# Attention, Fourier mixing and a feed-forward layer on one core: clearing tiles behind the fourth head, loading mask rows first, and copying kept columns in one step

## The chip, the core and the metric

The kernel runs on one core of a Trainium2 chip. A core has five engines with instruction streams of their own: TensorE (PE in the profile) multiplies matrices, and the loads of its stationary operand are listed apart as PEld; VectorE (DVE), ScalarE (ACT) and GpSimd (POOL) do elementwise work; SyncE (SP) only issues transfers. Each engine works through its own stream in order. Transfers between the device's memory and the on-chip memory are carried by 16 DMA engines; here they are issued from the streams of SP, ACT and POOL. The metric is the time of one execution on the device in microseconds; lower is better.

## The reference

Softmax attention with a block-causal mask over 8 batches of 8 heads, 576 positions of 64 columns; then a Fourier mixing over positions and over the 512 columns, of which the real part is added to the input; then a normalization and a feed-forward layer with 2048 hidden units:

```python
scores = scale * np.matmul(q, k.transpose(0, 1, 3, 2))
mask = block_i >= block_j                      # blocks of 64 positions
scores = np.where(mask, scores, -1000000000.0)
attn = np.exp(scores - np.max(scores, axis=-1, keepdims=True))
attn = attn / (np.sum(attn, axis=-1, keepdims=True) + 1e-09)
attn_out = np.matmul(attn, v)
...
x = np.ascontiguousarray(attn_out.transpose(0, 2, 1, 3)).reshape(B, S, H * D)
X = np.fft.fft(x, axis=1)
X = np.fft.fft(X, axis=2)
u = x + np.real(X)
mu = np.mean(u, axis=-1, keepdims=True)
var = np.mean((u - mu) ** 2, axis=-1, keepdims=True)
un = (u - mu) / np.sqrt(var + 1e-06)
out = u + np.maximum(un @ w_ch1, 0.0) @ w_ch2
```

q, k and v have the shape (8, 8, 576, 64); w_ch1 is 512 x 2048, w_ch2 is 2048 x 512; everything is float32.

## The kernel before

**How precision is kept.** Most products are made of two half-precision parts of each operand, a high and a low one. The weights' parts are made on the chip: the weights are loaded as they are (tile `W`, lines 1403 to 1427), DVE takes their bits apart in three passes (`weight_single`, line 1430), ACT sums their squares into a spare tile called `left` for a scale, and later steps scale and split them.

**The lanes and the planner.** The kernel is written as lanes of steps (`Step`, line 160): one lane loads heads, others prepare them, find maxima, make scores, make values, transform a finished batch, load the weights, and so on. A step has a function that emits instructions, a TensorE cost, a chain of the engines that it uses with a modelled cost of each, the steps that it must come after, and a place. A planner at the end (lines 1609 to 1675) picks steps in turn, keeps a model of when each engine is free (`Queue`, line 179; a step is booked in the first gap that its cost fits in) and emits each part of a step at its modelled start. The streams follow this order exactly, since every instruction is kept in program order (`Ordered`, line 203, and `mm`, line 245). So each stream's order is fixed when the kernel is built, and modelled costs decide it.

**A head.** For a head h, the transposed queries and keys stand in a tile `lead` (rows 0 to 63), below them nine more rows: eight mask rows and one row for the maxima. For the first two heads (`HF` = 2) this is `LEAD[h]`, whose rows 64 to 72 are loaded from `c_masks` by POOL's queue at line 317. `max_part` (line 659) multiplies over 72 rows, DVE reduces the maxima into `M`, `shift` (line 717) turns them by a product with the identity `ident`, ACT copies the result into `mt`, and SP's queue writes it into row 72 of `lead`. `scores` (line 747) then multiplies over 73 rows, so that mask and maximum are part of the product. ACT makes the exponentials `p` and their high part `ph`, POOL the low part `pl`; `values` (line 779) multiplies them with v, and DVE divides by the sums `DEN` (lines 815 to 820). A score step of a head needs parts of the values of the head before it (line 837).

**A batch.** When the eight heads of a batch are through, `fourier_steps` (line 873) transforms it. `mirror` loads the batch's rows as they are (`X`) and mirrored (`U`); `folded` adds and subtracts halves; `stage1` (line 943) multiplies with the cosine and sine tables over positions into tiles `z`; `stage1_tail` does one more column into `ZT`. The second stage, `stage2_sin` and `stage2_cos` (lines 987 and 1004), works on three pieces c = 0, 1, 2 of the transformed positions. Pieces 0 and 1 have 128 positions each and read the `z` tiles. Piece 2, the last 33 positions, is made for two batches at once: every batch copies its last columns of `z` and `ZT` into the kept tiles `ZP` and `ZTP`, at column offset `o`, 0 for even and 64 for odd batches (lines 961 and 979). Every odd batch then runs piece 2 for both batches, from `ZP` and `ZTP`, into `X2` and `U2`. The columns between the two batches' parts in the kept tiles are zero; they are cleared once, at the start: `X2` and `U2` by POOL (lines 312 and 313), `ZTP` and the eight halves of `ZP` by DVE (lines 323 to 326).

After the second stage `normalized_steps` (line 1080) normalizes 256 rows at a time and turns them, and `feed_steps` (line 1168) runs the feed-forward layer, which TensorE works on whenever no lane has a step ready.

**The tables.** `table_lane` (line 1601) loads the Fourier tables in four pieces, behind the values of heads 1, 2, 4 and 5 (`TABLES = (1, 2, 4, 5)`, line 45). Heads are counted from 0.

Of the kernel before, what the change touches and what calls it, by code (L numbers as in the profile page):

```python
# [9 lines left out]
F32 = mybir.dt.float32  # L10
# [3 lines left out]
AF = mybir.ActivationFunctionType  # L14
ALU = mybir.AluOpType
# [4 lines left out]
B, H, S, D = 8, 8, 576, 64  # L20
# [12 lines left out]
HF = 2  # L33
# [11 lines left out]
TABLES = (1, 2, 4, 5)  # L45
# [18 lines left out]
KS = KM + 1  # L64
# [155 lines left out]
def tile_attn_fourier_ffn(  # L220
# [31 lines left out]


    ident_r = const.tile([P, P], F32R, name="ident")
    gpsimd.dma_start(ident_r, c_id)
    ident = ident_r.bitcast(F32)
    rows = const.tile([P, 3], I32, name="rows")
    sync.dma_start(rows, c_rows)
    ones = const.tile([P, P], F32, name="ones")
# [4 lines left out]
    o = [0]  # L264
# [39 lines left out]
    VH = [const.tile([P, 5, 2, D + 1], F16, name=f"VH_{i}") for i in range(2)]  # L304
    VL = [const.tile([P, 5, 2, D], F16, name=f"VL_{i}") for i in range(2)]
    ZT = const.tile([P, NCOS], F32R, name="ZT")
    for i in range(2):
        gpsimd.memset(MAIN[i], LEAST)
        gpsimd.memset(MAIN[i][0:64, 0:1], 0.0)
        gpsimd.memset(DIAG[i], LEAST)  # L310
    X2, U2 = (const.tile([P, DM], F32, name=x) for x in ("X2", "U2"))
    gpsimd.memset(X2, 0.0)
    gpsimd.memset(U2, 0.0)
    ZP = {(name, m): const.tile([P, 2, width], F32R, name=f"zp{name}{m}") for name, width in (("c", 98), ("s", 96)) for m in range(2)}
    ZTP = const.tile([P, 98], F32R, name="ztp")
    for i in range(HF):
        gpsimd.dma_start(LEAD[i][D:KS], c_masks)
        vector.tensor_scalar(LEAD[i][0:D, 0:64], ones[0:D, 0:64], 0.0, None, op0=ALU.mult)
    for i in range(2):
        vector.memset(VH[i][:, 0:4, :, D:D + 1], 1.0)  # L320
        vector.memset(VH[i][0:64, 4, :, D:D + 1], 0.0)
        vector.memset(VH[i][64:128, 4, :, D:D + 1], 1.0)
    vector.tensor_scalar(ZTP, ones[:, 0:98], 0.0, None, op0=ALU.mult)
    for t in ZP.values():
        for x in range(2):
            vector.tensor_scalar(t[:, x], ones[:, 0:t.shape[2]], 0.0, None, op0=ALU.mult)
    for at in range(0, NCOS, P):
        w = min(P, NCOS - at)
        vector.tensor_scalar(ZT[:, at:at + w], ones[:, 0:w], 0.0, None, op0=ALU.mult)
# [543 lines left out]
    def fourier_steps(b):  # L873
# [59 lines left out]
        z = {}  # L933
# [9 lines left out]
        def stage1(name, m):  # L943
            mat, stack, k2, n = MATS[name]
            f0, f1, f2 = (fs[name, c] for c in range(3))
            ds = slice(P * m, P * (m + 1))
            t = ps_tile()
            i = 0
            for c, f in enumerate((f0, f1)):
                for a, w in ((0, 0), (1, 0), (0, 1)):  # L950
                    mm(t[:, 0:n], f[:, a, ds], mat[:, c, w], start=(i == 0), stop=False)
                    i += 1
            mm(t[:, 0:n], f2[0:k2, ds], stack[0:k2], start=False, stop=True)
            yield
            zz = z[name, m] = ztile(name, m).rearrange("p (x n) -> p x n", x=2)
            scalar.copy(zz[:, 0], t[:, 0:n])
            yield
            vector.tensor_tensor(zz[:, 1], t[:, 0:n], zz[:, 0].bitcast(F32), op=ALU.subtract)
            yield
            w = 33 if name == "c" else 32  # L960
            scalar.copy(ZP[name, m][:, :, o:o + w], zz[:, :, 256:256 + w].bitcast(F32))
            yield

        def stage1_tail():
            mat, stack, k2, n = MATS["c"]
            f0, f1, f2 = (fs["c", c] for c in range(3))
            t = ps_tile()
            i = 0
            for c, f in enumerate((f0, f1)):
                for w in range(2):  # L970
                    mm(t[0:2, 0:n], f[:, :, LDH], mat[:, c, w], start=(i == 0), stop=False, skip_group_check=True)
                    i += 1
            mm(t[0:1, 0:n], f2[0:k2, LDH:LDH + 1], stack[0:k2], start=False, stop=True, skip_group_check=True)
            yield
            scalar.copy(ZT[0:2], t[0:2, 0:n])
            yield
            vector.tensor_tensor(ZT[32:34], t[0:2, 0:n], ZT[0:2].bitcast(F32), op=ALU.subtract)
            yield
            scalar.copy(ZTP[:, o:o + 33], ZT[:, 256:289].bitcast(F32))
            yield  # L980

        bss = {}
# [4 lines left out]
        def stage2_sin(c):  # L987
            n = 128 if c < 2 else 96
            t = ps_tile()
            i = 0  # L990
            ns = slice(P * c, P * c + n)
            for m in range(2):
                for a, w in ((0, 0), (0, 1), (1, 0)):
                    lhs = z["s", m][:, a, ns] if c < 2 else last("s", m, a)
                    mm(t[0:n, 0:KCOL], lhs, sd[:, m, w], start=(i == 0), stop=(i == 5))
                    i += 1
            yield
            bs = bss[c] = work.tile([P, KCOL], F32, name="bs", bufs=1)
            if c == 2:
                gpsimd.memset(bs[96:97], 0.0)  # L1000
            scalar.copy(bs[0:n], t[0:n, 0:KCOL])
            yield

        def stage2_cos(c):
# [27 lines left out]
        D_ = lambda *a: ("d", b) + a  # L1032
        place = H * (b + 0.9)
        yield Step(
            mirror, 0.0, ("L3.0", "P3", "L2.5"), (("V", H * b + H - 1, 4),) + ((("F", feed_number(b - 2, 1)),) if b > 1 else ()), D_("u"),
            place=place,
        )
        def folds(name, op, width):
# [6 lines left out]
        def stages(name):  # L1045
            for m in range(2):
                yield Step(
                    lambda m=m: stage1(name, m), 0.87, ("A0.42", "D0.47", "A0.25"), (D_("f" + name),),
                    D_("z" + name) if m == 1 else None, True, place=place,
                )  # L1050
            if name == "c":
                yield Step(stage1_tail, 0.62, ("A0.4", "D0.46", "A0.23"), (D_("fc"),), D_("zt"), True, place=place)

        cos, sin = ("c", ALU.add, 257), ("s", ALU.subtract, 256)
        order = (folds(*cos), folds(*sin), stages("c"), stages("s"))
        for steps in order:
            yield from steps
        def second_stage(c):
            yield Step(lambda: stage2_sin(c), 0.67, ("A0.38",), (D_("zs"),), D_("b", c), True, place=place)
            yield Step(  # L1060
                lambda: stage2_cos(c), 0.78, ("D0.86", "B", "G3.0"), (D_("zc"), D_("zt"), D_("b", c)) + ((("F", feed_number(3, 2)),) if c == 2 and b == 5 else ()), D_("u", c), True,
                place=place,
            )

        for c in range(2):
            yield from second_stage(c)
        uu = tuple(D_("u", c) for c in range(3))
        yield from normalized_steps(low, uu[0:2], (store(b, 0), store(b, 1)), place)
        if b % 2:
# [84 lines left out]
    def feed_number(b, i):  # L1154

        return 2 * b + 1 + b // 4 + i
# [435 lines left out]
    def load_table(i):  # L1592

        ends = (0, 4 * NCOS, 4 * NCOS + 4 * NSIN, 5 * NCOS + 5 * NSIN + 4 * KCOL, c_dft.shape[1])
        lo, hi = ends[i], ends[i + 1]
        vector.tensor_scalar(dft[0:1, lo:lo + 1], DEN[i % 2][0:1, 0:1], 0.0, None, op0=ALU.mult)
        yield
        gpsimd.dma_start(dft[:, lo:hi], c_dft[:, lo:hi])
        yield

    def table_lane():
        for i in range(4):
            yield Step(lambda: load_table(i), 0.0, ("D0.15", "P1.0", "M2.3"), (("V", TABLES[i], 4),), ("dft", i), place=TABLES[i])

    def transform_lane():
# [114 lines left out]
```

## Time and profile before

| What | Value |
|---|---|
| median of 3 runs | 1207.31 us |
| lowest and highest of them | 1205.13 us, 1212.7 us |
| the profiled execution | 1204.48 us |
| its span in the profile | 1202.3 us |
| mean granted clock of TensorE over it | 0.965 of full speed |

The span is the time from the first to the last recorded instruction. In the lines of the profile, a line in order of time gives the start, the duration, the engine, the source line, the operation, what it writes and reads, and how many instructions are merged in it; in brackets stand the idle time of the engine before it and what ended that idle time. A line with L213 or L246 names a helper through which all instructions of an engine go, so the tiles' names tell what the work is. A waiting table's line says who waited for whom: microseconds in all, how often, and the longest. In a line on one tile, the three numbers after the count are the shortest, median and longest duration in nanoseconds, then come the first and the last start. A queue's line gives packets, megabytes and the time of its packets as a share of the 16 DMA engines: q1 is SP's queue, q10 ACT's, q0 POOL's. An issue of a transfer ("DMA_DIRECT2D") is the time of the issuing engine alone, not of the transfer. POOL's durations are rough.

### The profile page before, as it was taken

The page shows a single profiled execution, that of the slowest core. Times are in us where ns is not written, and L with a number is a line of the kernel's source. Part 1 is how long each engine was busy: PE and PEld are TensorE (multiplying, and loading weights), DVE is VectorE, ACT ScalarE, POOL GpSimd, SP SyncE. Part 2 cuts the span into 40 slices and gives each one's busy share as a digit, 9 for nine tenths or more (in the row PEclk, how much of TensorE's full clock was granted, in tenths as well). Part 3 has the DMA queues.
Part 4 walks back from the last instruction along what each step waited for, and adds up shares of the span by engine and source line. Part 5 has one row for each costly group of instructions (what it writes and reads, how often), then busy time and mean ns, then how long its engine had stood idle before and what let it go on. Part 6 is the DMA issues. An engine that isn't in the chain of part 4 may idle for free.

```text
span 1202.3 us, 26143 instructions
## 1 busy us (share of the span) xinstructions
PE 1122.9 (93%) x10182; PEld 824.4 (69%) x10182; DVE 741.8 (62%) x1616; ACT 630.8 (52%) x1374; POOL 475.6 (40%) x621
## 2 busy tenths in 40 slices
PE   4767799998789999999999999999999999999998
PEld 3544475675566777777776767677766766888875
DVE  6886876557857576666665566666656434454431
ACT  5666759757756566556574654675222212334320
POOL 4552414544653254425442533353334210455410
PEclk9956989999889999999999999999999999999999
DMA  9687233443444234543435422360122021011100
GB/s 259 194 253 233 105 106 87 121 124 103 123 115 103 76 87 106 113 132 81 123 99 142 126 82 82 91 151 14 32 43 56 23 60 30 28 36 26 28 19 18
DMA packets 94049, 115.07 MB, mean 96 GB/s; under 512 B 37591, under 2 KB 64129, under 8 KB 93926
## 3 DMA queue, kind: packets, MB, share of 16 engines
q1 hardware_dynamic: 86582, 89.06, 28.2%
q10 hardware_dynamic: 4384, 16.78, 4.3%
q0 software_dynamic: 2960, 7.58, 2.3%
q8 instruction: 80, 1.31, 0.5%
q14 instruction: 43, 0.35, 0.1%
HBM read 58.50 MB, written 18.89 MB: 64 GB/s over the span
## 4 chain that ended last, share of the span: by engine, by line
PE 70%; DVE 1%; DMA 1%; ACT 0%; SPq 0%; issue 0%; POOL 0%; DVEq 0%; ACTq 0%; POOLq 0%
PE acc L246 24%; PE ps L246 23%; PE h L246 17%; PE av L246 6%; DMA lead<-mt 1%; DMA rest<-lead 0%; SPq L213 0%; DVE p L213 0%; PE ps L249 0%; DVE M L213 0%; DVE gl L213 0%; ACT p L213 0%; DVE st L213 0%; DVE x L213 0%; PE h L249 0%
## 5 line engine op out<-in xcount | busy, mean ns | idle before, releaser
L213 POOL TENSOR_TENSOR pl<-p,ph 128x288 f16<-128x288 f32 (+1 forms) x256 | 261.0, 1029 | 345.6 <-ACT ph L213 188.3
L246 PEld LDWEIGHTS <-W 128*128 128x128 f16 x3456 | 332.5, 98 | 60.4 <-issue 1.5
L246 PE MATMUL acc<-W,gh 128*128 128x512 f16 (+1 forms) x1008 | 289.5, 369 | 1.5 <-DVE W L213 1.2
L246 PE MATMUL ps<-uh,W 128*128 128x256 f16 x1184 | 217.6, 273 | 0.0
L246 PE MATMUL h<-uh,W 128*128 128x256 f16 x1120 | 207.7, 275 | 0.0
L246 PE MATMUL acc<-W,gl 128*128 128x512 f16 (+1 forms) x504 | 186.2, 370 | 1.0 <-DVE gl L213 1.0
L246 PE MATMUL ps<-ul,W 128*128 128x256 f16 x592 | 161.2, 272 | 0.0
L246 PE MATMUL h<-ul,W 128*128 128x256 f16 x560 | 153.8, 275 | 0.1
L246 PEld LDWEIGHTS <-ph 128*128 128x128 f16 x2112 | 132.4, 102 | 27.1 <-issue 4.6
L246 PEld LDWEIGHTS <-gh 128*128 128x128 f16 x1056 | 98.8, 98 | 69.5 <-issue 1.8
L246 PE MATMUL av<-VH,pl 128*128 128x65 f16 (+1 forms) x963 | 117.2, 201 | 19.1 <-POOL pl L213 16.4
L213 DVE TENSOR_REDUCE M<-ps 128x1 fp32r<-128x320 f32 (+4 forms) x214 | 96.1, 483 | 59.7 <-PE ps L246 53.9
L246 PE MATMUL ps<-lead 73*128 73x288 f16 (+10 forms) x494 | 115.9, 295 | 14.1 <-DMA lead<-in_c_masks_dram 10.3
L246 PE MATMUL av<-VH,ph 128*128 128x65 f16 (+1 forms) x966 | 119.2, 202 | 3.2 <-DVE x L213 2.6
L246 PEld LDWEIGHTS <-pl 128*128 128x128 f16 x1056 | 102.9, 101 | 24.4 <-POOL pl L213 20.4
L246 PE MATMUL av<-VL,ph 128*128 128x64 f16 x960 | 117.4, 200 | 0.0
L213 ACT ACTIVATE gh<-ps 128x512 f16<-128x512 f32 x74 | 44.0, 594 | 114.8 <-PE ps L246 114.8
L213 ACT CAST ph<-p 128x512 f16<-128x512 f32 (+1 forms) x188 | 98.3, 523 | 5.1
L213 DVE SCALAR_TENSOR_TENSOR gl<-ps,gh 128x512 f16<-128x512 f32 x74 | 50.8, 688 | 80.3 <-ACT gh L213 79.9
L213 ACT ACTIVATE p<-ps 128x288 f32<-128x288 f32 (+1 forms) x159 | 79.4, 500 | 30.1 <-PE ps L246 26.5
L246 PEld LDWEIGHTS <-gl 128*128 128x128 f16 x528 | 51.5, 98 | 58.9 <-DVE gl L213 2.4
L246 PEld LDWEIGHTS <-lead 73*128 73x128 f16 (+1 forms) x744 | 64.9, 103 | 34.5 <-issue 6.1
(295 smaller groups left out, 1948.8 us busy)
## 6 DMA issues: line engine op xcount, KB each, us to landing
raw<-in_qk_dram SPq DMA_DIRECT2D x30, 576.0 KB
W<-in_moe_w_ch_dram ACTq DMA_DIRECT2D x14, 1024.0 KB
V<-in_v_dram SPq DMA_DIRECT2D x32, 320.0 KB
rest<-lead SPq DMA_DIRECT2D x64, 144.0 KB
rest<-rest SPq DMA_DIRECT2D x60, 144.0 KB
out_dram<-u SPq DMA_DIRECT2D x32, 256.0 KB
xd<-x SPq DMA_DIRECT2D x30, 256.0 KB
lead<-lead SPq DMA_DIRECT2D x60, 72.0 KB
```

Of the source, the lines that this page charges most:

```text
L213: x = f(*args, **kw)
L246: return tc.keep_in_program_order(nc.tensor.matmul(*args, **kw))
```

## The change

There are four edits.

1. At the start, POOL's queue issues the mask rows of the first two heads first and the identity behind them, then the small fills of `MAIN` and `DIAG`. Before, the identity came first, then the fills, then the masks.
2. The clearing of `X2`, `U2`, `ZTP` and `ZP` leaves the start. A new step `clear` does it: two fills on POOL, and nine writes on ACT (a copy of ones with scale 0) instead of DVE. It stands in the table lane ahead of the fourth table, after the values of head 4, with a modelled ACT cost of 2.2 us. The mirrors of the first two batches wait for it.
3. The five copies into `ZP` and `ZTP` leave `stage1` and `stage1_tail`. A new step `save` makes all five in one go on ACT, issued behind the second stage's pieces 0 and 1, with a modelled ACT cost of 1.25 us; it waits for `clear`, and piece 2 waits for it.
4. The modelled chains of `stage1` and `stage1_tail` lose the cost of the copies, so the planner takes these steps to be done sooner.

```diff
     ident_r = const.tile([P, P], F32R, name="ident")
-    gpsimd.dma_start(ident_r, c_id)
...
+    for i in range(HF):
+        gpsimd.dma_start(LEAD[i][D:KS], c_masks)
+    gpsimd.dma_start(ident_r, c_id)
     for i in range(2):
         gpsimd.memset(MAIN[i], LEAST)
...
-    gpsimd.memset(X2, 0.0)
-    gpsimd.memset(U2, 0.0)
...
     for i in range(HF):
-        gpsimd.dma_start(LEAD[i][D:KS], c_masks)
         vector.tensor_scalar(LEAD[i][0:D, 0:64], ones[0:D, 0:64], 0.0, None, op0=ALU.mult)
...
-    vector.tensor_scalar(ZTP, ones[:, 0:98], 0.0, None, op0=ALU.mult)
-    for t in ZP.values():
-        for x in range(2):
-            vector.tensor_scalar(t[:, x], ones[:, 0:t.shape[2]], 0.0, None, op0=ALU.mult)
...
-            w = 33 if name == "c" else 32
-            scalar.copy(ZP[name, m][:, :, o:o + w], zz[:, :, 256:256 + w].bitcast(F32))
-            yield
...
-            scalar.copy(ZTP[:, o:o + 33], ZT[:, 256:289].bitcast(F32))
             yield
...
-            mirror, 0.0, ("L3.0", "P3", "L2.5"), (("V", H * b + H - 1, 4),) + ((("F", feed_number(b - 2, 1)),) if b > 1 else ()), D_("u"),
+            mirror, 0.0, ("L3.0", "P3", "L2.5"), (("V", H * b + H - 1, 4),) + ((("F", feed_number(b - 2, 1)),) if b > 1 else (("clear",),)), D_("u"),
...
-                    lambda m=m: stage1(name, m), 0.87, ("A0.42", "D0.47", "A0.25"), (D_("f" + name),),
+                    lambda m=m: stage1(name, m), 0.87, ("A0.42", "D0.47"), (D_("f" + name),),
...
-                yield Step(stage1_tail, 0.62, ("A0.4", "D0.46", "A0.23"), (D_("fc"),), D_("zt"), True, place=place)
+                yield Step(stage1_tail, 0.62, ("A0.4", "D0.46"), (D_("fc"),), D_("zt"), True, place=place)
...
-            yield Step(lambda: stage2_sin(c), 0.67, ("A0.38",), (D_("zs"),), D_("b", c), True, place=place)
+            yield Step(lambda: stage2_sin(c), 0.67, ("A0.38",), (D_("zs"),) + ((D_("save"),) if c == 2 else ()), D_("b", c), True, place=place)
...
+        def save():
+            for name, w in (("c", 33), ("s", 32)):
+                for m in range(2):
+                    scalar.copy(ZP[name, m][:, :, o:o + w], z[name, m][:, :, 256:256 + w].bitcast(F32))
+            scalar.copy(ZTP[:, o:o + 33], ZT[:, 256:289].bitcast(F32))
+            yield
+
         for c in range(2):
             yield from second_stage(c)
+        yield Step(save, 0.0, ("A1.25",), (D_("zs"), D_("zc"), D_("zt"), ("clear",)), D_("save"), place=place)
...
+    def clear():
+        gpsimd.memset(X2, 0.0)
+        gpsimd.memset(U2, 0.0)
+        scalar.activation(ZTP, ones[:, 0:98], AF.Copy, scale=0.0)
+        for t in ZP.values():
+            for x in range(2):
+                scalar.activation(t[:, x], ones[:, 0:t.shape[2]], AF.Copy, scale=0.0)
+        yield
+
     def table_lane():
         for i in range(4):
+            if i == 3:
+                yield Step(clear, 0.0, ("A2.2",), (("V", TABLES[i] - 1, 4),), ("clear",), place=TABLES[i] - 1)
             yield Step(lambda: load_table(i), 0.0, ("D0.15", "P1.0", "M2.3"), (("V", TABLES[i], 4),), ("dft", i), place=TABLES[i])
```

More of the change, by code (lines that the diff above doesn't have):

```diff
@@ L977, in stage1_tail @@
             vector.tensor_tensor(ZT[32:34], t[0:2, 0:n], ZT[0:2].bitcast(F32), op=ALU.subtract)
-            yield
-            scalar.copy(ZTP[:, o:o + 33], ZT[:, 256:289].bitcast(F32))
             yield
```

## The prediction

> **What bounds the kernel now.** I read the page first (busy shares, slices, chain), then a table of stretches, then the order of time at the start and around the fourth head, then the transfers there.
>
> ```profile
> span 1202.3 us, 26143 instructions
> ...
> PE 1122.9 (93%) x10182; PEld 824.4 (69%) x10182; DVE 741.8 (62%) x1616; ACT 630.8 (52%) x1374; POOL 475.6 (40%) x621
> ...
> PE 70%; DVE 1%; DMA 1%; ACT 0%; SPq 0%; issue 0%; POOL 0%; DVEq 0%; ACTq 0%; POOLq 0%
> ```
>
> ```profile
> 0.00:20.00 20.00, 5.61 (x19) 4.42 (x19) 12.41 (x48) 8.48 (x14) 7.02 (x19) 1.00 0.92 258
> 20.00:100.00 80.00, 58.77 (x515) 42.59 (x516) 64.31 (x133) 51.43 (x118) 41.49 (x45) 0.75 0.77 239
> 100.00:160.00 60.00, 42.78 (x218) 25.50 (x217) 46.95 (x85) 38.47 (x84) 20.00 (x31) 0.82 0.37 119
> 160.00:280.00 120.00, 115.03 (x1155) 81.51 (x1154) 78.47 (x184) 87.14 (x191) 52.94 (x53) 0.99 0.43 116
> 280.00:360.00 80.00, 64.50 (x690) 48.23 (x689) 59.07 (x143) 54.30 (x125) 42.38 (x52) 0.89 0.42 118
> 360.00:1100.00 740.00, 739.25 (x6800) 544.78 (x6799) 451.12 (x979) 366.17 (x800) 287.92 (x372) 1.00 0.31 79
> ```
>
> The columns of the second fence are stretch, length, then busy time of PE, weight loads, DVE, ACT and POOL, then granted clock, share and rate of the transfers. TensorE bounds the kernel from 360 us on: 739.25 of 740 us at clock 1.00, and the chain that ended last is 70% PE. Before that it has holes: 14.4 us in the first 20, 21.2 to 100, 17.2 to 160, 5.0 to 280, 15.5 to 360. A change off TensorE can only be worth something in those 73 us, and whatever it does to ACT, POOL or DVE after 360 us is covered by PE. The amount of matrix work is the same before and after.
>
> **The change part by part.**
>
> *Masks first.* The first matrix work waits for the masks' rows:
>
> ```profile
> 1.26 0.80 POOL L213 DMA_DIRECT2D ident<-in_c_id_dram  x1 [0.82 <-POOLq L1702]
> ...
> 2.65 0.53 POOL L213 MEMSET X<- 128x512 f32 x1
> ...
> 3.12 0.52 POOL L213 MEMSET U<- 128x512 f32 x1
> ...
> 3.59 1.06 POOL L213 DMA_DIRECT2D lead<-in_c_masks_dram  x2
> ...
> 5.07 1.15 ACT L213 CAST lead<-raw 64x1152 fp32r<-64x1152 f32 x1 [3.06 <-DMA raw<-in_qk_dram]
> 5.07 0.14 DVE L213 COPY W<-raw 1x1 f32<-1x1 f32 x1 [0.94 <-DMA raw<-in_qk_dram]
> ...
> 10.34 1.62 PE L246 MATMUL ps<-lead 72*128 72x64 f32 x5 [10.34 <-DMA lead<-in_c_masks_dram]
> ...
> 13.74 0.27 PE L246 MATMUL acc<-ident,M 128*5 128x128 f32 x1 [1.13 <-DVE M L213]
> ```
>
> Their transfers move from 3.59 to the head of POOL's queue, where the identity's now starts at 1.26. With the delay that they have now (3.59 to 10.34, 6.75 us) matrix work could start at 8.0. It cannot start before the cast of the first head, 5.07 + 1.15 = 6.2. Nearest for a transfer issued at 1.26 is the identity's own. POOL's queue is q0; its packets stand first in the stretch from 3.5 to 5 us, then in that from 7.5 to 9:
>
> ```profile
> q0 software_dynamic: 144, 0.07, 42.7%
> ...
> q0 software_dynamic: 64, 0.09, 25.7%
> ```
>
> The first are the identity, moved by 5; the second the masks, moved by 9 and waited for until 10.34, 1.3 us later. So masks in the identity's place are there by some 6.3, with the cast. I take 6.2: the first matmul comes 4.1 us earlier, at least 2.3. What is late next at that point is the cast, which waits for the first head's load. The identity moves behind two mask issues (1.06 us): issued at 2.3, and with the same 6.75 us landed at 9.1; its first reader, 13.74 now, comes at 9.6 at the earliest, so it is covered by half a microsecond. SP's queue keeps its order. The small fills that POOL had before the masks now come after them, ahead of POOL's next work, which waits for the cast anyhow. The nine fills taken from DVE stood ahead of work that waits for a load until 5.07 (0.94 us idle): worth nothing.
>
> *What becomes of 4.1 us.* Follow it to the first scores:
>
> ```profile
> 12.87 0.38 ACTq L213 DMA_DIRECT2D W<-in_moe_w_ch_dram  x1
> ...
> 15.56 0.25 ACT L213 ACTIVATE mt<-acc 5x128 fp32r<-5x128 f32 x1
> ...
> 15.83 0.86 SPq L213 DMA_DIRECT2D lead<-mt  x1
> ...
> 18.38 0.69 DVE L213 TENSOR_SCALAR W<-W 128x1024 int32<-128x1024 int32 x1
> ...
> 20.53 0.61 PE L246 MATMUL acc<-lead 73*128 73x288 f32 x1 [1.76 <-DMA lead<-mt]
> ...
> 21.18 0.44 PE L246 MATMUL acc<-lead 73*128 73x288 f32 x1
> ...
> 21.62 1.06 ACT L213 ACTIVATE left<-W 128x1024 f16<-128x1024 f32 x1 [1.69 <-DVE W L213]
> ...
> 22.67 0.39 ACT L213 ACTIVATE ph<-acc 128x288 f16<-128x288 f32 x1
> ```
>
> The maxima, their turn and the issue of the maxima's row (15.83) move up by about 3 us: the full 4.1 is cut because ACT's work ahead of it reads loads that are still landing (transfers are 0.92 busy to 20 us). But the row then lands only at 20.53, 4.7 us after its issue, and the transfers show why:
>
> ```profile
> 17.00:19.00 2.00, 0.79 (x2) 0.37 (x2) 1.90 (x8) 0.71 (x2) 0.00 (x0) 1.00 1.01 365
> ...
> DMA packets 178, 0.73 MB, mean 365 GB/s; under 512 B 0, under 2 KB 0, under 8 KB 178
> ...
> q10 hardware_dynamic: 178, 0.73, 101.2%
> ```
>
> From 17 to 19 us all 16 engines move only the second weight load (ACT's queue, issued at 12.87), though the row, issued before 17 on SP's queue, is outstanding. The weight load is issued after the maxima too, so both move up together and the row stays behind it. The same bytes at the same rate give the same 20.53: at this point I book nothing. What does come through is on ACT: the first exponential (22.67) waits for the sum over the first weight load (21.62), and that for DVE's three passes over it (from 18.38). DVE reaches them about 3 us earlier, the sum is out of the way at 20, and the exponential starts with its matmuls at 21.2 to 21.3: 1.4 us. Heads run one behind the other to 100 us (DVE 64.31 of 80 busy), so I carry 1.4 us to the point where PE fills. Bounds: 0 (the heads after it wait for transfers, 0.77 busy) and 4.1.
>
> [...]
>
> *The clears.* Two POOL fills (0.53 and 0.52 above) and nine ACT writes of 96 or 98 columns go behind head 4's values. No such ACT write is in the trace; nearest are 66 columns at 0.243 us and 258 at 0.364 to 0.375:
>
> ```profile
> L213 ACT CAST zpc<-zc x16: 242/243/249, 120.0 to 1022.4; 128x66 fp32r<-128x66 f32 x16
> ...
> L213 ACT COPY bs<-ps x11: 364/375/375, 128.9 to 1056.5; 128x258 f32<-128x258 f32 x8, 96x258 f32<-96x258 f32 x3
> ...
> 72.69 0.19 DVE L213 RECIPROCAL rec<-DEN 128x5 f32<-128x5 f32 x1
> ...
> 74.81 0.82 ACT L213 ACTIVATE VH<-V,vacc 128x640 f16<-128x640 f32 x1
> ...
> 79.74 1.06 ACT L213 ACTIVATE left<-W 128x1024 f16<-128x1024 f32 x1 [4.11 <-DVE W L213]
> ...
> 81.57 0.72 POOL L213 TENSOR_TENSOR pl<-p,ph 128x288 f16<-128x288 f32 x1 [4.38 <-ACT p L213]
> ```
>
> Between them by width, 0.263 each, 2.4 us (2.2 to 3.4). Head 4's values end at 72.7 (row of the reciprocal). ACT then has work to 75.6 and stands idle for 4.11 us to 79.74, POOL 4.38 us to 81.57. The step is booked into the first gap of its length, so I put it there: 0. Gone that cover, it costs 2.4 us on ACT, and 1.05 beside it on POOL. It adds a wait in front of the first mirror, whose gathers sit on SP's and POOL's queues; but the mirror also waits for head 7's values, three heads further on, so that wait ends last.
>
> *The kept columns.* Five ACT copies a batch (0.243 and less, about 1.2 us) leave the first stage and follow the second stage's two pieces. The sum on ACT is unchanged; from the third batch on PE covers it. In the first two batches the copies leave a path that PE waits on and enter one just behind it: 0, within 1.2 either way. The copies' first reader, the second batch's third piece, comes after a whole normalization; the first stage's tiles, held longer by the copies, are next written by the first feed or a batch later.
>
> **Sum.** The profiled execution took 1204.48 us, 2.2 around its span. 1204.48 - 1.4 + 0 + 0 = 1203.1. It lies 2.8 below the median of the runs (1207.31), so the forecast for the median is 1205.9.
>
> **The rivals.**
>
> *Turns between the queues.* If the row does overtake, scores start about 3 us earlier: 1204.48 - 3.1 = 1201.4, as median 1204.2. For it: the row is tiny. Against: the 17 to 19 stretch.
>
> *Gain swallowed.* The later heads wait for weights and loads as before, or the masks land as late as before: 1204.5, median 1207.3. For it: transfers are 0.77 busy to 100 us. Against: PE and ACT wait for DVE there, not for weight loads.
>
> *The clears in the way (the slower one).* The nine writes land not in the 4.11 us gap but ahead of the write at 74.81, which DVE's next pass waits for. From the point where more than 1.4 of the 2.4 us lies ahead of such a write, the kernel is slower: 1204.48 - 1.4 + 2.4 = 1205.5, median 1208.3. For it: head 4's values end 2 us before that write. Against: the planner wants a free gap of 2.2.
>
> *Another order.* The first stage's chains are shorter for the planner, and two steps are new, so from head 5 on it writes out another order. In the holes up to 360 us, single waits come or go with the order:
>
> ```profile
> PE h L246 <- DMA fs<-add: 2.9, 1, 2.9
> ...
> PE h L246 <- DMA lead<-mt: 2.9, 1, 2.9
> ...
> PE h L246 <- DMA rest<-lead: 1.9, 1, 1.9
> ```
>
> Those three gone, or three new like them, are 7.7 us: 1195.4 or 1210.8, median 1198.2 or 1213.6. Nothing in the trace gives its sign.
>
> **How the numbers follow.** Forecast 0.36, turns 0.14, swallowed 0.13, clears 0.11, another order 0.26 (0.14 faster, with the start's gain behind it, 0.12 slower). The forecast's own range is 1203.2 (4.1 gained) to 1207.3. One per cent (12 us) is about what a measurement here can tell from no change. Only another order reaches past it, with more than its three waits; there are 73 us of holes to draw on, and I let about half of each side go so far: faster 0.08, slower 0.06, same 0.86. The range to give holds the first four and the other half of the last: 1197 to 1213.
>
> **What would show it.** First matmul at 6 to 8 us, released by the cast, not the masks; the maxima's row issued near 13 but scores still near 20.5 (near 17.5 if queues take turns); first exponential near 21.3; the clears as ACT work inside a gap near 76 us, PE no later for it; five copies in one run behind each second stage; 360 us on as before but shifted. Wrong if scores start early, if the write at 74.81 comes behind the clears, or if the holes between 100 and 360 us change by more than 3 us in sum.

## The result, and the profile after

| | before | after |
|---|---|---|
| median | 1207.25 us (9 runs) | 1197.84 us (9 runs, 1194.43 to 1202.28) |
| ratio, with its 95% interval | | 0.992, 0.9903 to 0.9937 |
| the profiled execution, its span | 1204.48 us, 1202.3 us | 1194.43 us, 1192.6 us |
| mean granted clock of TensorE | 0.965 | 0.987 |

The kernel became 9.4 us faster. The forecast was 1205.9 (a gain of 1.4 us) in a range of 1197 to 1213: the sign and the range held, the size did not. The profiled execution of the changed kernel is the fastest of its nine and has the highest clock of them (0.957 to 0.987), so the traces show somewhat more than the medians. The head of its page, then the table of the same stretches as before, from 100 us on:

```profile
span 1192.6 us, 26123 instructions
...
PE 1116.1 (94%) x10182; PEld 820.3 (69%) x10182; DVE 744.6 (62%) x1607; ACT 629.0 (53%) x1383; POOL 479.6 (40%) x621
```

```profile
100.00:160.00 60.00, 41.05 (x219) 25.41 (x218) 45.55 (x85) 40.24 (x87) 20.56 (x31) 0.83 0.36 114
160.00:280.00 120.00, 115.17 (x1197) 83.10 (x1196) 88.17 (x194) 84.56 (x193) 54.67 (x53) 1.00 0.39 110
280.00:360.00 80.00, 71.62 (x753) 52.75 (x751) 59.05 (x146) 55.97 (x127) 44.30 (x54) 0.94 0.47 129
360.00:1100.00 740.00, 732.67 (x6775) 541.30 (x6774) 447.01 (x969) 364.92 (x801) 291.51 (x377) 1.00 0.30 78
```

The number of matmuls is the same (10182). Two stretches stand out. From 280 to 360 us TensorE's holes fell from 15.5 us to 8.4, and the granted clock rose from 0.89 to 0.94. From 360 to 1100 us they rose, from 0.75 us to 7.3. So much was won before 360 us, and part of it was given back behind.

The start, in order of time:

```profile
1.25 1.28 POOL L213 DMA_DIRECT2D lead<-in_c_masks_dram  x2 [0.81 <-POOLq L1711]
...
6.18 1.65 PE L246 MATMUL ps<-lead 72*128 72x64 f32 x5 [6.18 <-ACT lead L213]
...
8.74 0.39 ACTq L213 DMA_DIRECT2D W<-in_moe_w_ch_dram  x1
...
9.69 1.11 SPq L213 DMA_DIRECT2D rest<-lead  x2
...
11.91 0.86 SPq L213 DMA_DIRECT2D lead<-mt  x1
...
18.54 1.06 ACT L213 ACTIVATE left<-W 128x1024 f16<-128x1024 f32 x1 [1.68 <-DVE W L213]
19.88 0.61 PE L246 MATMUL acc<-lead 73*128 73x288 f32 x1 [4.19 <-DMA lead<-mt]
20.53 0.41 ACT L213 ACTIVATE ph<-acc 128x288 f16<-128x288 f32 x1 [0.83 <-PE acc L246]
```

The first matmul came 4.2 us earlier, released by the cast and no longer by the masks. The row of maxima was issued 3.9 us earlier (15.83 to 11.91), but the scores that wait for it started only 0.65 us earlier (20.53 to 19.88). The first exponential came 2.1 us earlier. The clears, on ScalarE:

```profile
72.45 0.82 ACT L213 ACTIVATE VH<-V,vacc 128x640 f16<-128x640 f32 x1
73.17 0.27 ACT L213 ACTIVATE ztp<-ones 128x98 fp32r<-128x98 f32 x1
...
77.38 1.06 ACT L213 ACTIVATE left<-W 128x1024 f16<-128x1024 f32 x1 [2.56 <-DVE W L213]
```

The nine writes, of which the first is shown, stand behind the write of `VH` and in front of an idle time that is still 2.56 us long.

The largest difference is where the feed-forward layer resumes. In both kernels the second feed's last product runs at 287.6 us; no feed has rows until the second batch is transformed, normalized and turned. The first product of the third feed, before and after:

```profile
337.84 0.27 PE L246 MATMUL h<-uh,W 128*128 128x256 f16 x1
```

```profile
313.43 0.27 PE L246 MATMUL h<-uh,W 128*128 128x256 f16 x1
```

TensorE was without a feed for 50 us before and for 26 after. The stretches from the end of the second feed on, before and then after:

```profile
280.00:306.00 26.00, 21.10 (x268) 14.94 (x266) 22.68 (x54) 19.87 (x46) 12.41 (x12) 1.00 0.42 116
306.00:367.00 61.00, 50.39 (x496) 38.24 (x496) 41.47 (x100) 38.51 (x87) 34.69 (x44) 0.86 0.43 117
```

```profile
280.00:306.00 26.00, 20.47 (x173) 14.06 (x171) 20.21 (x45) 17.91 (x46) 14.62 (x19) 0.85 0.43 121
306.00:367.00 61.00, 58.15 (x649) 43.59 (x647) 43.88 (x110) 42.34 (x91) 34.33 (x40) 0.98 0.48 129
```

Busy time times granted clock is an estimate of how much TensorE did, in microseconds at full clock (the clock is a mean over busy and idle time alike). In the trace of before, 128x256 products in a row start 0.11 us apart at a clock of 1.00 (346.38, 346.49) and 0.21 us apart at 0.50 (358.59, 358.80). So it did 50.39 x 0.86 = 43.3 us before and 58.15 x 0.98 = 57.0 after, from 306 to 367 us. That is 13.7 us more in the same 61 us, more than the whole gain; from 280 to 306 us it did 3.7 us less (20.47 x 0.85 = 17.4 against 21.1). The end gives a second count: the span is 9.7 us shorter although there are 6.6 us more of holes behind 360 us, so by then the changed kernel was some 16.3 us ahead, of which some 2.4 come from the start.

### The profile page after: what moved, and what is told of

The parts are those of the page before. It is cut to its first block, busy times and chain, and to the rows that moved or that the text cites. A ratio compares the mean times of both kernels' runs of the same rounds, so it can differ in the third digit from the quotient of the medians.

```text
span 1192.6 us, 26123 instructions
## 1 busy us (share of the span) xinstructions
PE 1116.1 (94%) x10182; PEld 820.3 (69%) x10182; DVE 744.6 (62%) x1607; ACT 629.0 (53%) x1383; POOL 479.6 (40%) x621
## 4 chain that ended last, share of the span: by engine, by line
PE 80%; DMA 5%; DVE 5%; POOL 3%; ACT 3%; issue 2%; SPq 0%; DVEq 0%; ACTq 0%; POOLq 0%
PE acc L246 28%; PE ps L246 26%; PE h L246 19%; PE av L246 7%; DMA lead<-mt 3%; POOL pl L213 2%; DVE W L213 1%; DMA lead<-rest 1%; POOL u L213 1%; DVE M L213 1%; ACT p L213 1%; ACT ph L213 1%; POOL ag L213 1%; DMA fs<-add 0%; SPq L213 0%
## 5 line engine op out<-in xcount | busy, mean ns | idle before, releaser
L246 PE MATMUL h<-uh,W 128*128 128x256 f16 x1120 | 211.5, 275 | 4.9 <-DVE M L213 4.9
L246 PE MATMUL ps<-lead 73*128 73x288 f16 (+11 forms) x513 | 117.3, 293 | 13.6 <-ACT lead L213 6.2
L213 ACT ACTIVATE p<-ps 128x288 f32<-128x288 f32 (+1 forms) x166 | 82.5, 498 | 46.3 <-PE ps L246 38.5
```

What stands on the lines that cost most here:

```text
L213: x = f(*args, **kw)
L246: return tc.keep_in_program_order(nc.tensor.matmul(*args, **kw))
```

## The experiments

The theory: the gain is the masks at the start (some 2.5 us) and the planner's new order, in which the second batch's transform comes some 25 us earlier and the third feed with it (some 7 us). The clears and the copies by themselves are worth nothing. The rivals: the moved work itself pays; or the order pays in some other place.

| run | what it has | median us | before, run beside it | ratio, 95% interval |
|---|---|---|---|---|
| e1_masks | edit 1 alone | 1204.66 | 1207.9 | 0.9979, 0.9960 to 0.9998 |
| e2_order | the changed order, no work moved | 1201.15 | 1207.9 | 0.9939, 0.9916 to 0.9962 |
| e3_move | copies moved, order as before | 1208.4 | 1207.9 | 1.0005, 0.9985 to 1.0026 |
| e4_clear | edit 2 alone | 1206.32 | 1207.9 | 0.9978, 0.9957 to 0.9999 |
| e5_order_masks | the changed order and edit 1 | 1197.05 | 1209.16 | 0.9891, 0.9868 to 0.9914 |
| e6_hold | all edits, second transform held back | 1215.96 | 1209.16 | 1.0044, 1.0026 to 1.0061 |
| e7_early | before, planner looser for 8 heads | 1216.13 | 1209.16 | 1.0046, 1.0029 to 1.0063 |
| e8_masks_clears | edits 1 and 2 | 1205.42 | 1209.16 | 0.9977, 0.9957 to 0.9997 |
| e9_early_only | before, planner looser for one transform | 1201.8 | 1207.9 | 0.995, 0.9927 to 0.9973 |
| e10_row_queue | all edits, rows of maxima on another queue | 1193.4 | 1207.9 | 0.9879, 0.9852 to 0.9905 |
| e11_second_load | all edits, second weight load later | 1199.4 | 1207.9 | 0.9927, 0.9902 to 0.9951 |
| e12_early_row | e9 and e10's other queue, none of the edits | 1194.29 | 1207.04 | 0.9906, 0.9885 to 0.9927 |

### The parts alone

e1_masks takes the first edit's lines and nothing else; e4_clear the step `clear` and the mirrors' wait for it; e3_move puts the five copies behind the second stage's two pieces and leaves chains and steps as they were, so the order is that of before:

```diff
-            scalar.copy(ZP[name, m][:, :, o:o + w], zz[:, :, 256:256 + w].bitcast(F32))
...
         for c in range(2):
             yield from second_stage(c)
+        save()
```

e2_order does the opposite: the planner sees the shorter chains and a step of the same cost where `save` stands, but that step emits nothing, and the copies stay where they were, behind DVE's part of the first stage (TensorE's 10182 matmuls run in the order of the changed kernel; in e1_masks, e3_move and e4_clear they run in the order of before):

```diff
-                    lambda m=m: stage1(name, m), 0.87, ("A0.42", "D0.47", "A0.25"), (D_("f" + name),),
+                    lambda m=m: stage1(name, m), 0.87, ("A0.42", "D0.47"), (D_("f" + name),),
...
+        yield Step(lambda: iter((None,)), 0.0, ("A1.25",), (D_("zs"), D_("zc"), D_("zt")), D_("save"), place=place)
```

> Only the first edit: the masks' transfers ahead of the identity and the fills; clears and copies stay where they were, and the written order from the first head on is that of before. Theory O (the start gives 2 to 2.5 us, the rest of the gain comes from the new written order behind the first batch): first matmul near 6.2 us, head 7's values near 94.7 instead of 97.0, ratio near 0.998 (2.4 of 1207). Rival S (the start gives everything, 9.4 us, because the later stretches fall better once they begin earlier): ratio near 0.992. Rival N (the start's gain is lost by 290 us): ratio 1.000.

> The written order of the changed kernel without its work: the planner's chains of the first stage are shortened and a step of 1.25 us on ACT is booked behind the second stage's pieces 0 and 1, but it emits nothing; the five copies are still made in the first stage, the clears and the masks stay at the start. Theory O: second batch's first-stage tiles written near 280 us instead of 304, ratio near 0.994 (7 of 1207). Rival M (it is the five copies leaving the first stage's path that pays, not the order): ratio 1.000.

> The reverse of the one before: the five copies are made behind the second stage's pieces 0 and 1 on ACT, but no modelled cost is changed, so that everything else keeps the order of before. Theory O: ratio 1.000, within 0.001. Rival M: ratio near 0.994.

> Only the second edit: the clears behind head 4's values, on ACT and POOL; masks, copies and every modelled chain as before. Theory O: in the idle time of ACT, ratio 1.000, within 0.001. Rival C (clears in the way): 1.0 to 2.4 us slower, ratio 1.001 to 1.002.

The order alone gave 7.4 us by its ratio (0.0061 x 1207.9; 4.6 to 10.1), the masks alone 2.5 (0.2 to 4.8), the moved copies nothing. The two add up to 0.0082 of the time, and the whole change has 0.008. In e2_order the third feed starts early too, in spite of the start being that of before, and TensorE does 57.35 x 0.90 = 51.6 us of work from 306 to 367 us, 8.3 more than before:

```profile
318.03 0.27 PE L246 MATMUL h<-uh,W 128*128 128x256 f16 x1
```

```profile
306.00:367.00 61.00, 57.35 (x604) 42.33 (x605) 42.99 (x104) 42.75 (x93) 33.95 (x42) 0.90 0.48 129
```

The clears gave as much as the masks, which no theory had expected. The order of time in e4_clear shows how:

```profile
2.54 1.06 POOL L213 DMA_DIRECT2D lead<-in_c_masks_dram  x2
```

```profile
6.65 1.62 PE L246 MATMUL ps<-lead 72*128 72x64 f32 x5 [6.65 <-DMA lead<-in_c_masks_dram]
```

Without the fills of `X2` and `U2` in front of them, the masks are issued at 2.54 instead of 3.59, 1.05 us earlier, and the matmul that waits for them starts 3.7 us earlier (6.65, was 10.34). So the clears do at the start what the masks' edit does, in another way.

### Do the two add, and is it the order

e5_order_masks is e2_order with edit 1; e8_masks_clears is edits 1 and 2 without the copies and their order.

> The masks' edit and the changed kernel's order of steps, without its work: the clears stay at the start and the kept columns' copies stay in the first stage. Theory 'order and masks' (the start gives about 2.5 us, the order about 7, the moved clears and copies nothing of their own): ratio 0.992, as the whole change has it, with the second batch's first-stage casts near 278 us. Rival 'the clears are half the start' (the fills taken from the start add to the masks' edit): 0.994 to 0.995, 2 to 3 us behind the whole change.

> The masks' edit and the clears' edit together, with the kept columns' copies and the order as before. Each of the two alone gave 0.998. Theory 'one start' (both bring the masks' rows forward, and the row of maxima still waits behind the second weight load): ratio 0.9975 to 0.9985, no more than either alone. Rival 'they add': 0.995 to 0.996.

Masks and clears together gave 0.9977, no more than either alone: there is one start to be won. Order and masks gave 0.9891, with none of the clears' or copies' work moved; that is as much as the whole change (0.992; the intervals overlap, and the medians are 1197.05 and 1197.84). So neither the moved clears nor the moved copies are what pays.

### Is it the second batch's transform

The two orders first differ near 128 us, where the first batch's first stage ends; further on, the changed one has the second batch's folds ahead of the values of head 17, and the one before has them behind. e6_hold is the whole change with that wait added:

```diff
-                    lambda c=c: folded(op, width, name, c), 0.0, ("t1",) + (("X1.6", "A1.2", "X0.9") if c == 2 else ("X1.12", "A0.41", "X0.43")) + ("t",), (D_("u"),) + ((("F", 1),) if b == 1 else ()) + ((("t", feed_number(b - 1, 1), 1),) if b and name == "s" else ()),
+                    lambda c=c: folded(op, width, name, c), 0.0, ("t1",) + (("X1.6", "A1.2", "X0.9") if c == 2 else ("X1.12", "A0.41", "X0.43")) + ("t",), (D_("u"),) + ((("F", 1), ("V", 17, 4)) if b == 1 else ()) + ((("t", feed_number(b - 1, 1), 1),) if b and name == "s" else ()),
```

e7_early is the kernel before, with the limit on how far ahead an engine may be booked raised from 3 to 10 us for steps up to the second batch's place:

```diff
-                    return max(r, opening(engine, max(r, now), cost) - BACKLOG)
+                    return max(r, opening(engine, max(r, now), cost) - (BACKLOG if step.place > 16 else 10.0))
```

> The whole change, but the second batch's folds also wait for the values of head 17, which puts its transform back to about where it lay before, and changes nothing of the work. Theory 'early second transform' (feed 3 starts sooner because its rows are turned some 25 us earlier): the casts of its first stage come after 295 us, feed 3 ends near 400 us and the order's gain of some 7 us goes; the start's gain stays: ratio 0.997 to 0.999. Rival 'order elsewhere' (the gain is spread over the order's other differences): 0.992 to 0.994, with the casts late all the same.

> The kernel before, with one number of its planner changed: a step of the second batch's transform may be issued when its engine is booked up to 10 us ahead, instead of 3; none of the four edits is in it. Theory 'early second transform': the casts of the second batch's first stage come near 280 us instead of 304, feed 3 ends 15 to 20 us sooner, and the kernel is 4 to 8 us faster: ratio 0.993 to 0.997. Rival 'order elsewhere': the casts come early and the ratio is 0.999 to 1.002, as that time is given back in the feeds behind.

Holding the transform back took the gain away and more: 1.0044. The stretch and the third feed of e6_hold:

```profile
306.00:367.00 61.00, 53.16 (x547) 40.30 (x548) 37.52 (x88) 35.91 (x83) 36.49 (x45) 0.83 0.37 102
```

```profile
333.12 0.27 PE L246 MATMUL h<-uh,W 128*128 128x256 f16 x1
```

With the feed back at 333 us, TensorE does 53.16 x 0.83 = 44.1 us of work there, as before (43.3). That much is as the theory had it. What it had not is the loss of some 5 us against before (and the casts begin at 291.5 us, not after 295). TensorE's longest wait from 440 to 620 us, where before it waits for nothing, has a large part in it:

```profile
PE ps L246 <- DMA lead<-mt: 7.9, 2, 5.8
```

So e6_hold changes more than the transform's place, and its time by itself proves little.

e7_early missed: it became slower. But the edit did more than its expectation says. The limit was loosened for every step without TensorE work at the second batch's places, the preparation of its heads included, so the order changed from the ninth head on. Its TensorE holes from 160 to 280 us show what that cost:

```profile
160.00:280.00 120.00, 110.60 (x1076) 77.19 (x1075) 70.46 (x163) 78.70 (x172) 49.31 (x49) 0.95 0.35 96
```

They are 9.4 us (5.0 before), at 0.95 instead of 0.99 of the clock. It tells nothing on the transform by itself. e9_early_only loosens the limit for that transform alone:

```diff
-                    return max(r, opening(engine, max(r, now), cost) - BACKLOG)
+                    return max(r, opening(engine, max(r, now), cost) - (10.0 if abs(step.place - (2 * H - 0.8)) < 0.001 else BACKLOG))
```

> The kernel before, with the looser limit of 10 us for the steps of the second batch's transform alone; every other step keeps its limit of 3, so the order is that of before up to that transform, which the last such kernel's was not. None of the four edits is in it. Theory 'early second transform': casts of its first stage by 290 us, no loss ahead of them, 8 to 13 us of TensorE's work won by 367 us, part of it given back behind 450 us, and 2 to 8 us faster in all: ratio 0.993 to 0.998. Rival 'the order ahead of it' (what counts is the order of the head stage, and an early transform costs the heads as much as it gives the feeds): no gain by 367 us and a ratio of 1.000 or more.

It was faster, 0.995, with none of the change's four edits. Its first-stage casts come at 273 us, its third feed and its stretch:

```profile
313.50 0.27 PE L246 MATMUL ps<-uh,W 128*128 128x256 f16 x1
```

```profile
306.00:367.00 61.00, 59.41 (x644) 44.59 (x641) 37.61 (x94) 40.80 (x89) 32.42 (x40) 1.00 0.44 124
440.00:620.00 180.00, 172.41 (x1748) 125.21 (x1747) 117.40 (x275) 109.54 (x241) 77.40 (x91) 0.98 0.40 106
```

59.4 us of work there against 43.3: 16 us won. From 440 to 620 us it lacks 180 - 172.41 x 0.98 = 11.0 us, where before lacked none. So an earlier second transform pays by itself, about as much as the changed order does (0.995 and 0.9939), and most of what it wins can be lost again.

### What gives it back

From 440 to 620 us TensorE of the kernel before waits for nothing. The waiting tables of that stretch, for TensorE alone, of after and, the longest alone, of e9_early_only:

```profile
PE h L246 <- DMA lead<-mt: 2.8, 1, 2.8
PE ps L246 <- DMA lead<-rest: 1.6, 1, 1.6
PE ps L246 <- DVE M L213: 1.0, 1, 1.0
```

```profile
PE ps L246 <- DMA lead<-mt: 5.6, 1, 5.6
```

The longest is one row of maxima, 1.2 KB. In after, SyncE's queue at that point reads:

```profile
559.96 0.64 SPq L213 DMA_DIRECT2D left<-U  x1
560.65 0.82 SPq L213 DMA_DIRECT2D left<-X  x1
561.56 0.62 SPq L213 DMA_DIRECT2D left<-U  x1
...
563.43 0.73 SPq L213 DMA_DIRECT2D lead<-mt  x1
```

The scores that need the row start at 569.13, 5.7 us after its issue. What SyncE's queue, q1, moved from 566 to 567.4 us, just before:

```profile
q1 hardware_dynamic: 18, 0.04, 6.8%
```

These are 18 packets of some 2 KB, the length of a row of `left`, in 6.8% of the time of 16 engines, which is about the time of one engine (6.25%). So, as an estimate, the `left<-U` copies (31 rows each) go one row after the other through a single DMA engine, and the part of the row of maxima that falls to that engine waits behind them. The order decides whether a row is issued there: in e9_early_only and e6_hold one follows the last of these copies at once (563.84 behind 563.12, 577.36 behind 576.64), in the kernel before the next one is issued 15 us later (599.66 behind 584.48). No run changes the copies, so this cause is argued, not shown. In e6_hold the row ends a hole of 5.8 us (583.61). Two runs move only the row's queue, from the 25th head on, the first on the whole change and the second on e9_early_only:

```diff
-            sync.dma_start(both(h)[0][KM:KS, 0:640].rearrange("r (j p) -> r j p", j=5), mt)
+            (scalar if h >= 3 * H else sync).dma_start(both(h)[0][KM:KS, 0:640].rearrange("r (j p) -> r j p", j=5), mt)
```

> The whole change, with the rows of maxima of heads 24 and on issued from ScalarE's queue instead of SyncE's; the order of the steps is the same. Theory 'row behind the transfers' (the hole of 2.76 us before a scores matmul at 569 us is SyncE's queue with 128 KB copies and transposes in front of the row): the hole falls under 1 us, those of 474 and 528 us stay (they wait for others), and the kernel is 1.5 to 3 us faster than the whole change: ratio 0.989 to 0.991. Rival 'the engines behind the queues' (the row waits for the transfers wherever it is issued): the hole stays and so does 0.992.

> The kernel before, with the looser limit for the second batch's transform alone (as the last but two), and with the rows of maxima of heads 24 and on issued from ScalarE's queue. None of the four edits is in it. Theory 'the row gives it back': the hole of 5.56 us before a scores matmul at 571 us is gone or under 1 us, so that some 4 to 6 us more of what the early transform wins are kept: ratio 0.990 to 0.992. Rival 'given back anyway' (the TensorE work that the early transform won is lost at the next batch's transform in some other wait): the hole goes, others come, and the ratio stays at 0.994 to 0.996.

The waits of the same stretch, of e10_row_queue and, the longest alone, of e12_early_row:

```profile
PE ps L246 <- DVE M L213: 2.3, 2, 1.3
PE h L246 <- DMA lead<-mt: 1.4, 2, 1.0
```

```profile
PE ps L246 <- ACT p L213: 1.8, 1, 1.8
```

The long waits for the row are gone in both. e12_early_row went from e9_early_only's 0.995 to 0.9906, at the ratio that was expected (their intervals touch at 0.9927); others took a part (1.8 us for an exponential). e10_row_queue has the lowest median of all, 1193.4 us. It was not run beside the whole change: its ratio of 0.9879 (0.9852 to 0.9905) and the change's 0.992 (0.9903 to 0.9937) just touch, and in the traces TensorE is only 1.6 us busier from 440 to 620 us (176.23 against 174.64), so what the row's queue is worth on the whole change is not settled. Two small edits to the kernel before, one number of the planner and one queue, gave about as much as the change (1194.29 us).

### The row at the start

In e11_second_load the second weight load is issued behind the second head's row of maxima:

```diff
-        scalar.dma_start(raw(x).rearrange("p (j n) -> p j n", j=n), weight(i, n))
+        if x != 1:
+            send(x)
...
         sync.dma_start(dst.bitcast(F32), mt.bitcast(F32))
+        if h == 1:
+            send(1)
```

> The whole change, with the second weight load issued from ScalarE's queue behind head 1's row of maxima (near 15.5 us) instead of at 8.74; the order of the steps is the same. Theory 'row behind the load' (the first row, issued at 11.91, lands at 19.9 because the load's 1 MB is ahead of it): scores near 16 to 17, first exponential near 17, 2 to 4 us faster than the whole change if the later weights allow it: ratio 0.989 to 0.991. Rival 'the bytes ahead' (what delays the row are the operand copies of SyncE's own queue and the other loads): scores stay within 1 us of 19.9 and the ratio at 0.992 or a little above, as the load is late.

```profile
11.84 0.86 SPq L213 DMA_DIRECT2D lead<-mt  x1
...
15.41 0.38 ACTq L213 DMA_DIRECT2D W<-in_moe_w_ch_dram  x1
...
16.90 0.61 PE L246 MATMUL acc<-lead 73*128 73x288 f32 x1 [1.62 <-DMA lead<-mt]
...
18.13 1.06 ACT L213 ACTIVATE left<-W 128x1024 f16<-128x1024 f32 x1 [1.39 <-DVE W L213]
...
19.19 0.39 ACT L213 ACTIVATE ph<-acc 128x288 f16<-128x288 f32 x1
```

The row, issued at the same time (11.84), now releases the scores at 16.90 instead of 19.88: with the load behind it, it came 3 us sooner. How the load held it is seen in the queues, ScalarE's q10 and SyncE's q1. The changed kernel from 13 to 17 us:

```profile
q10 hardware_dynamic: 192, 0.77, 56.1%
q1 hardware_dynamic: 191, 0.64, 45.3%
```

e11_second_load from 13 to 15 us:

```profile
q1 hardware_dynamic: 209, 0.67, 98.9%
```

The load did not go ahead of the row as a whole. The two queues moved as many packets as each other (192 and 191), while SyncE's queue still had transfers to move that were issued ahead of the row, such as the copies at 9.69: by 17 us it had moved 2.49 MB, and 2.69 MB were issued ahead of the row. Without the load, SyncE's queue moved as many bytes in half the time (0.67 MB in 2 us, beside the load 0.64 in 4). From these counts I take it, as an estimate, that the row waited for what stood ahead of it on its own queue, at half that queue's rate. The kernel before has two microseconds, from 17 to 19, in which ScalarE's queue alone moved (178 packets, no other), though the row had been issued; no run shows why.

Yet the time did not follow (0.9927). The exponential came only 1.3 us earlier, since ScalarE first makes the sum over the first weight load (18.13), and the fourth head's values end where they do in the whole change, at 57.5 us.

## Why the prediction was right or wrong

**Masks first: right.** The first matmul was forecast at 6.2, released by the cast; it came at 6.18, so released. Wrong beside it: the lower bound of 2.3 us took the masks' delay of 6.75 us as fixed, and the clears' leaving the start was given no worth. e4_clear shows that without POOL's two fills, 1.05 us, the first matmul comes 3.7 us earlier. It changed no sum, as the masks' edit takes the same time.

**What becomes of 4.1 us: right outcome, mis-sized, and for a reason that was half right.** The row's issue moved by 3.9 us, not 3, and its scores stayed near 20 us because of the second weight load; e11_second_load confirms that (16.90 with the load behind the row, 19.88 with it ahead). But the load did not fill all 16 engines, as was read from the stretch of 17 to 19 us: after the change, from 13 to 17 us, the two queues moved 192 and 191 packets, and other transfers stood ahead of the row on SyncE's queue. The rival of turns between the queues had scores 3 us earlier, where 0.65 us was measured; no run shows such turns themselves, only these equal counts, and the rival left out the row's own queue. The rival of the gain swallowed falls, as the heads keep the gain. The sum over the weight load moved by 3.1 us and was out of the way, as forecast; the exponential came at 20.53 and not at 21.2 to 21.3 because the scores that it waits for came 0.65 us earlier, where the prediction booked nothing. The term of 1.4 us should have been 2.1 at that point; at the eighth head's values it was 2.4 (97.04 before, 94.67 after), and e1_masks measured 2.5.

**The clears and the kept columns: right.** The clears went into the gap by the write of `VH` that the forecast named, and e8_masks_clears with e1_masks puts them at nothing. e3_move puts the copies at nothing. The slower rival, clears in the way, did not come about: the write of `VH` stands in front of them.

**Another order: the step that failed.** The prediction carried 0 for it, gave it a chance of 0.26, sized it by three single waits of some 2.5 us and said "Nothing in the trace gives its sign". e2_order measured 7.4 us, faster. Not the three waits made it but a stretch: TensorE without a feed from 287.6 to 337.84 us, of which the prediction had counted the holes (15.5 us from 280 to 360) without asking what would fill them. That the sign follows from a modelled chain made shorter was not shown by the trace; that TensorE had no feed for 50 us there, and that an earlier second transform would end it, could have been read from it. Luck had its part: the faster side of this rival was put at 1198.2, next to the measured 1197.84, but from three waits that are not what moved (that of 2.9 us for `fs<-add` is still there with 2.8), and the range to give holds the result by 0.84 us. By its own test the prediction was wrong here: the holes from 100 to 360 us fell from 37.7 to 32.2 us, by 5.5 where 3 was allowed.

**"360 us on as before but shifted": wrong.** With feeds earlier, heads and the fourth batch's transform met in another way, and TensorE got 7.3 us of holes in the stretch where it had 0.75. One of these waits, for the row of maxima, belongs to the order and not to the moved work: e9_early_only, which moves none, has it too, and e10_row_queue and e12_early_row end it by another queue. Not tried: what makes the other two waits, other copies into `left`, and which of e7_early's steps cost it the heads.

## What to carry to other kernels

Where a planner writes the order, an edit of a modelled cost is an edit of the order: look for the longest stretch in which the bounding engine has no filler work, and price what moves its end. When TensorE is full behind such a stretch, a gain there is worth what the later waits leave of it, so look next at the small transfers that TensorE waits for, and at what is issued ahead of them on their queue. Two edits that both bring the same first transfer forward were not worth their sum here (0.9979 and 0.9978 alone, 0.9977 together).

## What the runs showed of the hardware

Behind one of two holes TensorE had half its clock for some microseconds, behind the other it had all of it. The stretches around the row's hole, of after (2.76 us, ended at 569.13) and of e9_early_only (5.56 us, ended at 571.09), where the third number from the end is the granted clock:

```profile
566.00:569.00 3.00, 0.37 (x3) 0.10 (x1) 1.06 (x2) 1.12 (x2) 1.31 (x3) 1.00 0.29 75
569.00:575.00 6.00, 5.87 (x71) 4.64 (x71) 1.92 (x5) 4.25 (x9) 2.78 (x4) 1.00 0.00 0
```

```profile
566.00:571.00 5.00, 0.00 (x0) 0.00 (x0) 1.15 (x3) 0.34 (x1) 1.62 (x2) 0.76 0.66 179
571.00:575.00 4.00, 3.91 (x18) 2.62 (x18) 0.06 (x1) 1.94 (x5) 1.52 (x3) 0.50 0.63 195
```

Behind the hole of 2.76 us the clock stays at 1.00; behind that of 5.56 us the next 4 us run at 0.50, so that, as an estimate (half of these 4 us), the hole cost some 2 us more than it lasted. In e6_hold, with a hole of 5.8 us that ends at 583.61, the clock is at 0.50 from 580 to 586 us. Length alone does not tell such holes apart: in the kernel before, one of 2.92 us that ends at 356.14 has 0.50 behind it, from 357 to 360 us, and in e12_early_row the clock is at 0.50 from 572 to 574 us, behind a hole of 1.8 us. The prediction counted holes by their length alone: of the 13.7 us won from 306 to 367 us, 7.8 are busy time and the rest is the clock, 0.86 before and 0.98 after. The clock is not fixed by the order alone, though: with the same order, e2_order has 0.90 there, and over their whole spans the nine runs of the changed kernel have 0.957 to 0.987.

A load of another queue held a small transfer here: the scores that wait for 2.5 KB on SyncE's queue started 3 us sooner (16.90 instead of 19.88) when a load of 1 MB on ScalarE's queue was issued behind it (e11_second_load), though its own issue had not moved (11.84 and 11.91). With the load ahead, the two queues had moved 191 and 192 packets from 13 to 17 us, and SyncE's queue took these 4 us for 0.64 MB, where without it 2 us were enough for 0.67 MB.
